# First logits of a fused attention and two-layer expert kernel moved to another PSUM bank and to the end of a pair's scores, and half of the first loads issued by ScalarE

## The chip, the cores and the metric

The kernel runs on one core of a Trainium2 chip. The metric is the time of one execution in microseconds (us), as the device measures it; the kernel before has a median of 680.31 us over 3 runs (679.55 to 680.96).

## What is computed

Three stages follow each other; everything is float32.

```python
# q, k, v: (4, 12, 448, 64): 4 batches, 12 heads, 448 tokens
scores = matmul(q, k.transpose(0, 1, 3, 2)) / sqrt(64) - log(448)
x = matmul(1 / (1 + exp(-scores)), v)          # sigmoid attention
x = x.transpose(0, 2, 1, 3).reshape(1792, 768)
x = ((x @ w_a) * (x @ w_b)) @ w_out            # 768 -> 1536 -> 768
logits = x @ phi                               # (1792, 32): 8 experts, 4 slots each
d = softmax(logits, axis=0)                    # over the tokens
slots = d.T @ x                                # (32, 768)
y = relu(slots @ w1[e]) @ w2[e]                # per expert e
c = softmax(logits, axis=1)                    # over the slots
out = c @ y
```

## The kernel before, in words

**Work.** Two heads make a pair, so there are 24 pairs `g`, six to a batch. For each pair `load_qkv` (lines 120 to 151) loads k, q and v; k and q are transposed and split into a high and a low part (`emit_TK`, `emit_TQ`), on TensorE for the early pairs (line 170, evicted by VectorE and ScalarE) and on VectorE from pair 13 on (line 166). `emit_S` (197 to 212) computes scores in four chunks of 112 keys, each chunk as two PSUM tiles (one per head) with three matmuls each; ScalarE turns each tile into a sigmoid (line 211). `emit_PV` (216 to 222) multiplies the eight sigmoid tiles of a pair with v in sixteen matmuls, and `emit_x` evicts the result (on ScalarE, line 244, from batch 1 on).

**Order.** Nothing is scheduled by a compiler: each engine runs its instructions in the order in which the code issues them. `att` (253 to 294) is the generator that sets that order for attention. For pair 12 and later it emits: the k/q split of pair `g + 1`; chunk 0 of pair `g`; the PV product of pair `g - 1` and its eviction; then chunks 1, 2 and 3 of pair `g`. After every `yield` of `att` the main loop (1021 to 1029) lets one `fill_step` run, which advances a queue of filler generators by one step.

**The filler around the change.** When batch 0's product of the second stage is done, `first_LG` (868 to 878) is put into that queue. It transposes four 128 by 512 blocks on TensorE (`group`, line 529, evicted by VectorE at 531) and runs `LG(0)`: `logits(0)` (line 775) waits for the flag `run["done"]`, then emits one matmul that adds four partial logits (line 783), the maximum over the tokens (787, 793, VectorE), the exponential (802, ScalarE, which loads another table for it and the sigmoid's table again afterwards), a copy of the logits (807, VectorE); later steps transpose the two results (819, 825) and multiply the exponentials with the second stage's result (836, 96 matmuls).

**PSUM.** `ms` tiles (lines 64 to 68) are general tiles with 2 banks; score tiles have the tags `sc` (4 banks) and, for chunk 2, `ab` (2 banks). From pair 13 on (`GT0`) the first head's tile of chunk 0 is an `ms` tile; from pair 12 on the PV product's tile is one too.

**Start.** `load_qkv(0)` loads k and q of pair 0 head by head, all issued by SyncE (line 150), then v; then `consts` sets up constants; then pairs 1 and 2 are loaded. TensorE's first work is the transposes of k and q of pair 0 (line 170).

**End.** From about 480 us on the expert weights (48 MB) stream in through a ring of slots (line 979).

```python
for cost in att_g:
    if not run.pop("trans", False):
        fill_step()
    run.pop("done", None)
```

Of the kernel before, what the change touches and what calls it, by code (L numbers as in the profile page):

```python
# [18 lines left out]
B, H, S, D = 4, 12, 448, 64  # L19
DM, FF, NS, NE, F = 768, 1536, 32, 8, 1024  # L20
C = 4
# [14 lines left out]
def body(ctx, tc, q, k, v, w_a, w_b, w_out, phi, w1, w2, out):  # L36
    nc = tc.nc
    pe, act, dve, pool, sp = nc.tensor, nc.scalar, nc.vector, nc.gpsimd, nc.sync
# [15 lines left out]
    run = {}  # L54

    def ps_tile(tag, shape, bufs):
        return psp.tile(shape, F32, tag=tag, name=tag, bufs=bufs)
# [6 lines left out]
    def ms(shape=(128, S)):  # L64
        tags = banks[run["banks"]]
        tag = tags[run["ms"] % len(tags)]
        run["ms"] += 1
        return ps_tile(tag, list(shape), 4 if tag == "sc" else 2)
# [51 lines left out]
    def load_qkv(g, names):  # L120
        if g >= B * NP:
            return
        b, p = divmod(g, NP)
        for src, nm, n in ((k, "k", 3), (q, "q", 3), (v, "v", 3)):
            if nm not in names:
                continue

            if g >= GT0:
                if nm == "v":
                    t = atp.tile([T, 2, C, D], F32, tag="vn", name="vn", bufs=n)  # L130
                    sp.dma_start(out=t, in_=src[b, 2 * p:2 * p + 2].rearrange("h (c p) d -> p h c d", c=C))
                else:
                    t = atp.tile([128, 2 * C * D], F32, tag=nm + "n", name=nm + "n", bufs=n)
                    t = t[:, :S].rearrange("p (n d) -> p n d", d=32)
                    for j in range(4):
                        sp.dma_start(out=t[32 * j:32 * j + 32],
                                     in_=src[b, 2 * p + j // 2][:, j % 2 * 32:j % 2 * 32 + 32].rearrange(
                                         "(n t) d -> t n d", t=32))
                qkv_t[nm, g] = t
                continue  # L140
            s = src[b, 2 * p:2 * p + 2].rearrange(
                "h (c p) d -> p h c d" if nm == "q" else "h (p c) d -> p h c d", c=C)
            if nm == "v":
                t = atp.tile([T, 2, C, D], F32, tag="vn", name="vn", bufs=n)
                sp.dma_start(out=t, in_=s)
            else:
                t = atp.tile([128, 2 * C * D], F32, tag=nm + "n", name=nm + "n", bufs=n)
                t = t[:T].rearrange("p (c h d) -> p c h d", c=C, h=2)
                for h in range(2):
                    sp.dma_start(out=t[:, :, h], in_=s[:, h])  # L150
            qkv_t[nm, g] = t

    stk = {}
# [21 lines left out]
    def emit_TK(g):  # L175
        if g >= B * NP:
            return
        if g >= GT0:
            for nm in "kq":
                split_heads(g, nm, transposed(g, nm), dve.tensor_copy)  # L180
                load_qkv(g + 3, nm)
            return
        tk = transposed(g, "k")
        if not g:
            tq = transposed(g, "q")
        split_heads(g, "k", tk, dve.tensor_copy)
        if not g:
            split_heads(g, "q", tq, act.copy)

    def emit_TQ(g):  # L190
        if g >= B * NP:
            return
        split_heads(g, "q", transposed(g, "q"), dve.tensor_copy)
# [3 lines left out]
    def emit_S(g, chunks):  # L197

        (kh, kl), (qh, ql) = stk[g]["k"], stk[g]["q"]
        for c in chunks:  # L200
            ab = (g < NP or g > 2 * NP) and c == 2
            sc = [ms((T, S)) if g >= GT0 and c == 0 and not h else ps_tile("ab" if ab else "sc", [T, S], 2 if ab else 4)
                  for h in range(2)]
            cs = slice(c * T, (c + 1) * T)
            for i, (kx, qx) in enumerate(((kh, qh), (kl, qh), (kh, ql))):
                for h in range(2):
                    r = slice(64 * h, 64 * h + 64)
                    pe.matmul(sc[h], kx[r, cs], qx[r], start=(i == 0), stop=(i == 2))  # L208
            for h in range(2):
                a = atp.tile([T, S], F32, tag="a", name="a", bufs=11)  # L210
                act.activation(a, sc[h], AF.Sigmoid, bias=nlog[:T], scale=1.0 / math.sqrt(D))  # L211
                a_t[g, h, c] = a
# [3 lines left out]
    def emit_PV(g, cs):  # L216
        if cs[0] == 0:
            pv_t[g] = ps_tile("sc", [128, S], 4) if g < 2 * NP else ms()
        for c in cs:
            for h in range(2):  # L220
                pe.matmul(pv_t[g][64 * h:64 * h + 64], qkv_t["v", g][:, h, c, :], a_t.pop((g, h, c)),  # L221
                          start=(c == 0), stop=(c == C - 1))
# [15 lines left out]
    def emit_x(g):  # L238
        pv = pv_t.pop(g)
        qkv_t.pop(("v", g))  # L240
        b, kk = divmod(g, NP)
        if b:
            xt[g] = raw_x(b, kk)
            act.copy(xt[g], pv)
        else:
            xh = x0p.tile([128, S], F32R, tag=f"xh{kk}", name=f"xh{kk}")
            xl = x0p.tile([128, S], F32R, tag=f"xl{kk}", name=f"xl{kk}")
            act.activation(xh, pv, AF.Copy)
            dve.tensor_tensor(xl, pv, xh.bitcast(F32), op=ALU.subtract)
            xt[g] = (xh, xl)  # L250
        load_qkv(g + 3, "v")

    def att():

        emit_TK(0)
        yield 860
        for g in range(B * NP + 1):
            more = g < B * NP
            dense = g < NP or g >= 2 * NP
            first = ((0, 1) if g == 0 else (0, 2) if g == B * NP - 1 else (0,) if dense else ()) if more else ()  # L260
            if g:
                emit_TK(g + 1)
                yield 430
            for c in first:
                emit_S(g, (c,))
                run["done"] = True
                yield 800
            if g:
                if g < NP and more:
                    emit_TQ(g + 1)  # L270
                    yield 430
                emit_PV(g - 1, (0, 1, 2, 3))
                emit_x(g - 1)
                yield 3200
            else:
                emit_TK(g + 1)
                yield 430
            if not more:
                return
            if not dense:  # L280
                emit_S(g, (0, 1))
                yield 1600
                emit_TQ(g + 1)
                yield 430
                emit_S(g, (2, 3))
                yield 1600
            else:
                if not g:
                    emit_TQ(g + 1)
                    yield 430  # L290
                for c in range(C):
                    if c not in first:
                        emit_S(g, (c,))
                        yield 800

    PAIR = 860 + 4 * 800 + 3200
# [478 lines left out]
    def logits(b):  # L775
        while not b and not run.pop("done", False):
            yield
        if b == B - 1:
            project(b, 2, 3)
        lf = ms()  # L780
        if b == B - 1:
            pe.matmul(lf, wphi[:, :4].rearrange("p j s -> p (j s)"), gT[b, KF - 1], start=True, stop=False)
        pe.matmul(lf, selF.rearrange("p j s -> p (j s)"), lp[b], start=b < B - 1, stop=True)
        if b:
            yield
        mx = col()
        dve.tensor_reduce(mx, lf, axis=AX.X, op=ALU.max)
        nm = col()
        if b:
            mn = col()  # L790
            dve.tensor_tensor(mn, run["m"], mx, op=ALU.max)
            mx, m0 = mn, run["m"]
        dve.tensor_scalar(nm, mx, -1.0, None, op0=ALU.mult)
        if b:
            dm = col()
            dve.tensor_tensor(dm, m0, mx, op=ALU.subtract)
        run["m"] = mx
        if b:
            yield
        sm = col()  # L800
        ls, d = run["lsd"]
        act.activation(d, lf, AF.Exp, bias=nm, accum_out=sm)
        if b:
            al = col()
            act.activation(al, dm, AF.Exp)
            run["al"] = al
        (act.copy if b else dve.tensor_copy)(ls, lf)
        yield
        if b:
            sn = col()  # L810
            dve.scalar_tensor_tensor(sn, run["s"], al, sm, op0=ALU.mult, op1=ALU.add)
            sm = sn
        run["s"] = sm
# [290 lines left out]
    for what in order0:  # L1104
        i = what[1]
        h, n, f0 = (0, 4, 4 * i) if i < 3 else (1, 6, 6 * (i - 3))
# [18 lines left out]
    for n in range(0, len(order1), 4):  # L1125
        _, g, x, _ = order1[n]
# [51 lines left out]
    for h, (c0, w) in enumerate(COLS):  # L1178
# [4 lines left out]
        t = ms((128, w))  # L1183
# [41 lines left out]
```

## Time and profile before

| what | value |
|---|---|
| median of 3 runs | 680.31 us (679.55 to 680.96) |
| the profiled execution | 683.6 us, of which the span of the profile is 681.8 us |
| TensorE busy in the span | 639.4 us (94%) |
| VectorE / ScalarE / GpSimdE busy | 397.3 / 294.0 / 311.8 us |
| moved by DMA | 154.25 MB, 226 GB/s over the span |
| mean granted clock of TensorE | 0.983 of full speed |
| chain that ended last | TensorE 77%, DMA 13%, ScalarE 3%, VectorE 2%, issue 2% |

The profile is one execution. In its rows PE is TensorE's matmuls, PEld its weight loads, DVE is VectorE, ACT is ScalarE, POOL is GpSimdE, SP is SyncE; SPq and ACTq are the sequencers that issue DMAs. `L783` is line 783 of the kernel. A wait in brackets is idle time of the engine just before the row, with what ended it. The chain that ended last is followed back from the last instruction: at each step to what released it, or to the instruction before it on its engine. The 1.8 us between the span and the profiled execution lie outside of the profile.

### The profile page before, as it was taken

The page shows a single profiled execution, that of the slowest core. Times are in us where ns is not written, and L with a number is a line of the kernel's source. Part 1 is how long each engine was busy: PE and PEld are TensorE (multiplying, and loading weights), DVE is VectorE, ACT ScalarE, POOL GpSimd, SP SyncE. Part 2 cuts the span into 40 slices and gives each one's busy share as a digit, 9 for nine tenths or more (in the row PEclk, how much of TensorE's full clock was granted, in tenths as well). Part 3 has the DMA queues.
Part 4 walks back from the last instruction along what each step waited for, and adds up shares of the span by engine and source line. Part 5 has one row for each costly group of instructions (what it writes and reads, how often), then busy time and mean ns, then how long its engine had stood idle before and what let it go on. Part 6 is the DMA issues. An engine that isn't in the chain of part 4 may idle for free.

```text
span 681.8 us, 10900 instructions
## 1 busy us (share of the span) xinstructions
PE 639.4 (94%) x4035; PEld 455.0 (67%) x4035; DVE 397.3 (58%) x565; ACT 294.0 (43%) x531; POOL 311.8 (46%) x236
## 2 busy tenths in 40 slices
PE   6999999997999899999999999999999998996693
PEld 4556777775676455568998898898879895441131
DVE  4775899996994648929887767754233422210022
ACT  4888778776683568874333233201210002110021
POOL 0233677666773207819997675742344442000000
PEclk9999999999999899999999999999999999999888
DMA  9997999999997346310214242341999999999998
GB/s 192 278 275 190 289 308 304 282 274 295 288 293 198 71 83 115 60 48 3 91 47 115 79 101 93 102 124 40 280 382 366 403 370 332 412 414 417 405 354 276
DMA packets 150292, 154.25 MB, mean 226 GB/s; under 512 B 81792, under 2 KB 126688, under 8 KB 147168
## 3 DMA queue, kind: packets, MB, share of 16 engines
q1 hardware_dynamic: 145600, 151.61, 71.3%
q10 hardware_dynamic: 4640, 1.95, 1.1%
q8 instruction: 32, 0.52, 0.3%
q14 instruction: 20, 0.16, 0.1%
HBM read 126.36 MB, written 27.17 MB: 225 GB/s over the span
## 4 chain that ended last, share of the span: by engine, by line
PE 77%; DMA 13%; ACT 3%; DVE 2%; issue 2%; POOL 1%; SPq 0%; DVEq 0%; ACTq 0%; POOLq 0%
PE ab L565 24%; PE sc L745 15%; DMA e<-in_moe_w 8%; PE ab L745 8%; PE sc L208 6%; PE sc L221 5%; PE ms L221 4%; DMA out<-w 3%; PE ms L170 2%; PE ms L836 2%; PE ab L208 1%; PE ms L493 1%; ACT a L211 1%; DMA gkp<-in_moe_w 1%; PE sc L1193 1%
## 5 line engine op out<-in xcount | busy, mean ns | idle before, releaser
L367 POOL TENSOR_TENSOR w<-gk,cy 128x768 int32<-128x768 int32 x36 | 66.7, 1853 | 91.1 <-DVE gk L362 57.6
L211 ACT ACTIVATE a<-sc,sums 112x448 f32<-112x448 f32 x147 | 84.4, 642 | 12.2 <-PE sc L208 11.9
L565 PE MATMUL ab<-t,wh 128*128 128x448 f32 x288 | 65.1, 371 | 0.0
L565 PEld LDWEIGHTS ab<-t,wh 128*128 128x128 f32 x288 | 53.4, 188 | 6.1 <-issue 1.3
L463 POOL TENSOR_TENSOR wl<-wr,wh 128x768 fp32r<-128x768 f32 x16 | 29.5, 1841 | 49.9 <-DVE wh L462 25.7
L463 POOL TENSOR_TENSOR wl<-w,wh 128x768 fp32r<-128x768 f32 x24 | 47.0, 1960 | 2.5 <-ACT wh L462 2.5
L572 ACT COPY misc<-ab 128x448 f32<-128x448 f32 x24 | 12.7, 529 | 80.7 <-PE ab L565 80.7
L1156 PE MATMUL ab<-e,gk 128*32 128x384 f32 x240 | 33.1, 573 | 10.7 <-DMA e<-in_moe_w 10.6
L360 DVE TENSOR_SCALAR mf<-gk 128x768 f32<-128x768 f32 x36 | 34.0, 943 | 14.3 <-ACT gk L349 14.1
L221 PE MATMUL sc<-a,vn 112*64 112x448 f32 x192 | 39.1, 546 | 1.0 <-ACT a L211 1.0
L221 PE MATMUL ms<-a,vn 112*64 112x448 f32 x192 | 38.7, 545 | 0.2 <-ACT a L211 0.2
L575 DVE TENSOR_TENSOR misc<-misc,ab 128x448 f32<-128x448 f32 x24 | 14.7, 614 | 36.8 <-PE ab L565 36.8
L208 PE MATMUL sc<-qh,kh 64*112 64x448 f32 x147 | 35.4, 431 | 0.7 <-ACT qh L158 0.6
L565 PE MATMUL ab<-xh,wl 128*128 128x448 f32 x144 | 35.4, 383 | 0.0
L361 DVE TENSOR_SCALAR gk<-mf 128x768 uint32<-128x768 uint32 x36 | 34.3, 953 | 1.2
L565 PE MATMUL ab<-xh,wh 128*128 128x448 f32 x144 | 34.9, 378 | 0.0
L565 PE MATMUL ab<-xl,wh 128*128 128x448 f32 x144 | 34.5, 375 | 0.0
L565 PE MATMUL ab<-t,wl 128*128 128x448 f32 x144 | 34.3, 373 | 0.0
L629 POOL TENSOR_TENSOR wx<-wr,wx 128x384 fp32r<-128x384 f32 x29 | 32.3, 1115 | 3.5 <-ACT wx L628 3.4
L628 ACT CAST wx<-T 128x384 fp32r<-128x384 f32 x21 | 10.8, 513 | 53.4 <-DVE T L650 33.9
L629 POOL TENSOR_TENSOR wx<-T,wx 128x384 fp32r<-128x384 f32 x23 | 24.8, 1080 | 16.9 <-ACT wx L628 15.6
L1195 DVE COPY o<-sc 112x384 f32<-112x384 f32 x11 | 5.6, 551 | 46.0 <-PE sc L1193 45.9
(458 smaller groups left out, 1514.4 us busy)
## 6 DMA issues: line engine op xcount, KB each, us to landing
e<-in_moe_w SPq DMA_DIRECT2D x23, 1024.0 KB, 8.8
e<-in_moe_w SPq DMA_DIRECT2D x23, 768.0 KB, 15.1
wr<-ab SPq DMA_DIRECT2D x14, 768.0 KB, 4.6
ab<-w SPq DMA_DIRECT2D x24, 384.0 KB, 6.9
vn<-in_v SPq DMA_DIRECT2D x24, 224.0 KB, 4.1
gk<-gk SPq DMA_DIRECT2D x24, 224.0 KB, 4.6
e<-in_moe_w SPq DMA_DIRECT2D x14, 384.0 KB, 8.8
wr_cv<-in_moe_w_a SPq DMA_DIRECT2D x6, 768.0 KB, 7.4
```

Of the source, the lines that this page charges most:

```text
L208: pe.matmul(sc[h], kx[r, cs], qx[r], start=(i == 0), stop=(i == 2))
L211: act.activation(a, sc[h], AF.Sigmoid, bias=nlog[:T], scale=1.0 / math.sqrt(D))
L221: pe.matmul(pv_t[g][64 * h:64 * h + 64], qkv_t["v", g][:, h, c, :], a_t.pop((g, h, c)), start=(c == 0), stop=(c == C - 1))
L360: dve.tensor_scalar(mf, m, LOW, HIGH, op0=ALU.max, op1=ALU.min)
L361: dve.tensor_scalar(mi, mf.bitcast(U32), 3, 0x3FFFFFFF, op0=ALU.logical_shift_left, op1=ALU.bitwise_and)
L367: pool.tensor_tensor(thirds(w), m.bitcast(I32), thirds(cy_t.pop(x)), op=ALU.add)
L463: pool.tensor_tensor(wl, t, wh.bitcast(F32), op=ALU.subtract)
L565: pe.matmul(t, w[:, kk * 128:(kk + 1) * 128], xt[b * NP + kk][xi], start=(s == 0 and kk == 0), stop=(s == 2 and kk == KD - 1))
L575: dve.tensor_tensor(g, g, t, op=ALU.mult)
L629: pool.tensor_tensor(w[:, 1], t, w[:, 0].bitcast(F32), op=ALU.subtract)
L745: pe.matmul(t, w[:, wi, k * 128:(k + 1) * 128], xs[ORDER[m], k][xi], start=(s == 0 and k == 0), stop=(s == 2 and k == 2))
L1156: pe.matmul(sps[h][32 * j:32 * j + 32], hT[:, 2 * x + i, 2 * j + g], ring[order2[n + j]][0][:, i, c0:c0 + w], start=(g == 0 and x == 0 and ...
```

## The change

Two places. In `load_qkv`, for pair 0 alone, the second head's k and q are issued by ScalarE's DMA queue, the first head's by SyncE's as before. In the logits of batch 0, the PSUM tile is of the tag `ab` and no longer an `ms` tile, and the flag that `logits(0)` waits for is set after the last of chunks 1 to 3 (only then true) and no longer after the chunks that come ahead of the PV product.

```diff
                 for h in range(2):
-                    sp.dma_start(out=t[:, :, h], in_=s[:, h])
+                    (sp if g or not h else act).dma_start(out=t[:, :, h], in_=s[:, h])
...
             for c in first:
                 emit_S(g, (c,))
-                run["done"] = True
                 yield 800
...
                 for c in range(C):
                     if c not in first:
                         emit_S(g, (c,))
+                        run["done"] = c == C - 1
                         yield 800
...
-        lf = ms()
+        lf = ms() if b else ps_tile("ab", [128, S], 2)
```

What moves at the start, on SyncE (kn and qn are the tiles of k and q; a row with x2 is both heads):

```order
 L1221 UNCONDITIONAL_BRANCH
-L150 DMA kn<-in_k 112x4x64 x2
-L150 DMA qn<-in_q 112x4x64 x2
+L150 DMA kn<-in_k 112x4x64
+L150 DMA qn<-in_q 112x4x64
 L145 DMA vn<-in_v 112x2x256
 L150 DMA kn<-in_k 112x4x64 x2
```

SyncE issues two DMAs fewer ahead of v of pair 0 and of everything behind it; ScalarE issues the same two ahead of its first table load.

What moves on TensorE in pair 13, beside which `logits(0)` runs (L208 are scores, L221 the PV product of pair 12, L529 the block transposes, L783 the logits):

```order
 L208 MATMUL sc<-ql,kh 112x448
-L783 MATMUL ms<-misc,selF 128x448
 L221 MATMUL ms<-a,vn 64x448 x8
 L208 MATMUL sc<-qh,kh 112x448 x2
 L208 MATMUL sc<-qh,kl 112x448 x2
 L208 MATMUL sc<-ql,kh 112x448 x2
-L529 MATMUL ms<-ident,misc 128x128 x4
 L208 MATMUL ab<-qh,kh 112x448 x2
 L208 MATMUL ab<-qh,kl 112x448 x2
```

The logits matmul is gone from ahead of the PV product, and with it the four transposes that stood behind chunk 1. Where they stand now, with the waits of each row, between chunk 3 of pair 13 and the PV product of pair 13 (a_2545 is the first sigmoid tile of pair 13; ms_2632 and sc_2633 are chunk 0 of pair 14):

```order
L783 MATMUL ab_2606<-misc_95,selF_90 128x448 [waits DVE_49,Activation_49]
L208 MATMUL ms_2632<-qh_2524,kh_2514 112x448 [waits DVE_49,PE_49]
L208 MATMUL sc_2633<-qh_2524,kh_2514 112x448
...
L208 MATMUL sc_2633<-ql_2525,kh_2514 112x448
L529 MATMUL ms_2644<-ident_89,misc_95 128x128 [waits PE_49]
L529 MATMUL ms_2644<-ident_89,misc_95 128x128 x3
L221 MATMUL ms_2650<-a_2545,vn_2087 64x448 [waits DMAHW3_49,Activation_49]
```

The other transposes, the steps of lines 819 and 825 and the 96 matmuls of line 836 follow about a pair later than before, all still ahead of the PV product of pair 15, as before. On ScalarE the exponential moves with them (L211 are sigmoids, L244 the eviction of the PV product of pair 12):

```order
 L211 ACTIVATE a<-sc,sums 112x448
+L244 COPY r_2562<-ms 128x448
+L211 ACTIVATE a<-sc,sums 112x448 x2
+L211 ACTIVATE a<-ab,sums 112x448 x2
+L211 ACTIVATE a<-sc,sums 112x448 x2
 L802 ACT_TABLE_LOAD
-L802 ACTIVATE ls_d,sums<-ms,sums 128x448
-L244 COPY r_2568<-ms 128x448
+L802 ACTIVATE ls_d,sums<-ab,sums 128x448
 L211 ACT_TABLE_LOAD
```

Before, the two table loads stood ahead of the sigmoids of chunks 1 to 3 of pair 13, around the eviction of the PV product; now they stand behind those, and ahead of the sigmoids of chunk 0 of pair 14.

## Rows read from the trace of the kernel before

**Rows 1.** The page, busy time, share of the span and instructions of each engine.

```profile
PE 639.4 (94%) x4035; PEld 455.0 (67%) x4035; DVE 397.3 (58%) x565; ACT 294.0 (43%) x531; POOL 311.8 (46%) x236
```

**Rows 2.** Waits of TensorE, 0 to 240 us: us in total, times, longest us.

```profile
PE ms L170 <- ACT wT L393: 2.8, 3, 2.2
...
PE ms L170 <- DMA qn<-in_q: 0.2, 1, 0.2
PE ms L221 <- ACT a L211: 0.2, 1, 0.2
```

**Rows 3.** Timeline of SyncE, 0 to 14 us: start us, us, what.

```profile
0.73 1.36 SPq L150 DMA_DIRECT2D kn<-in_k  x2
2.14 1.15 SPq L150 DMA_DIRECT2D qn<-in_q  x2
```

**Rows 4.** The chain that ended last, 0 to 60 us: start us, us, what.

```profile
2.80 3.37 DMA qn<-in_q
...
6.30 0.99 PE ms L170 x4
...
15.77 0.54 PE ms L170 x4
```

**Rows 5.** Busy time by stretch at the start; last columns granted clock, DMA share, GB/s.

```profile
3.00:4.00 1.00, 0.00 (x0) 0.00 (x0) 0.00 (x0) 0.00 (x0) 0.00 (x0) 1.00 0.41 94
4.00:5.00 1.00, 0.00 (x0) 0.00 (x0) 0.00 (x0) 0.00 (x0) 0.00 (x0) 1.00 1.23 264
```

**Rows 6.** Timeline of TensorE, 220 to 234 us.

```profile
221.03 1.02 PE L783 MATMUL ms<-misc,selF 128*128 128x448 f32 x2 [1.23 <-ACT a L211]
221.97 3.23 PE L221 MATMUL ms<-a,vn 112*64 112x448 f32 x16
...
227.72 0.66 PE L529 MATMUL ms<-ident,misc 128*128 128x128 f32 x4 [1.72 <-ACT r L244]
...
230.20 1.97 PE L529 MATMUL ms<-ident,misc 128*128 128x128 f32 x8
```

**Rows 7.** Timeline of ScalarE, 218 to 232 us.

```profile
225.22 1.28 ACT L802 ACT_TABLE_LOAD   x1 [3.72 <-issue]
...
227.14 0.52 ACT L244 COPY r<-ms 128x448 f32<-128x448 f32 x1
227.68 1.28 ACT L211 ACT_TABLE_LOAD   x1
228.97 1.16 ACT L211 ACTIVATE a<-sc,sums 112x448 f32<-112x448 f32 x2
```

**Rows 8.** Busy time by stretch around the logits; third column from the end granted clock.

```profile
229.60:233.00 3.40, 3.40 (x18) 2.19 (x16) 1.49 (x3) 2.63 (x6) 2.11 (x2) 0.58 0.00 0
```

**Rows 9.** Timeline of an undisturbed pair, 250 to 257 us, TensorE and ScalarE.

```profile
250.14 3.23 PE L221 MATMUL ms<-a,vn 112*64 112x448 f32 x16
...
255.31 1.16 ACT L211 ACTIVATE a<-ab,sums 112x448 f32<-112x448 f32 x2
...
255.93 3.23 PE L221 MATMUL ms<-a,vn 112*64 112x448 f32 x16
256.34 1.18 ACT L211 ACTIVATE a<-sc,sums 112x448 f32<-112x448 f32 x2
```

**Rows 10.** The chain that ended last, 216 to 252 us: score chunks.

```profile
228.37 0.79 PE ab L208 x6
229.16 1.11 PE sc L208 x6
...
248.39 0.61 PE ab L208 x6
```

**Rows 11.** Busy time by stretch, 480 to 560 us; columns as in Rows 5.

```profile
480.00:560.00 80.00, 80.00 (x556) 67.57 (x556) 26.09 (x49) 6.76 (x15) 32.77 (x18) 1.00 1.02 365
```

**Rows 12.** The chain that ended last, over the whole span, two pieces.

```profile
122.55 8.95 DMA out<-w
...
590.32 11.05 DMA e<-in_moe_w
```

## Prediction

> **What bounds the kernel now.** I read the page first. TensorE is busy for 639.4 of 681.8 us [rows 1]: whatever keeps it waiting counts. Next come its waits up to 240 us: 2.8 us in three waits at the weight conversion [rows 2], and 1.2 and 1.7 us around the first logits, the brackets in its timeline [rows 6]. At the start it has nothing to do until k and q of pair 0 have landed [rows 4]. From there on the reader should see that nothing makes TensorE wait: it is busy for all of 480 to 560 us, while the DMA engines are full [rows 11], and from 590 us the chain is one load of expert weights after another [rows 12]. That stream starts when TensorE gets to its place in the program, so a microsecond won or lost before 480 us moves the end by one, and I count both places of the change in full.
>
> **The first loads.** SyncE takes 1.36 us to issue k and 1.15 us to issue q of pair 0 [rows 3]. The last of the four DMAs is issued at 2.80 and lands 3.37 us later, at 6.17; the transposes of q start at 6.30 [rows 4]. With two queues the second k is issued at 0.73 with the first, the second q at some 1.4. ScalarE's own first work, a table load and one activation, slips by 1.3 us, and the eviction that it has to be ready for comes 4 us later: no cost. Three estimates of the gain:
> - by latency: 2.80 - 1.4 = 1.4 us;
> - by bytes: the four loads are 458 KB. At 94 GB/s between 3 and 4 us the engines are fed slower than they work (0.41 busy), at 264 GB/s one microsecond later they are full [rows 5]. With two issuers the 264 GB/s are there from the first byte, at some 2.2 us: 458 KB by 3.9 us in place of 4.9, so 1.0 us;
> - by TensorE: the transposes of k, as long as q's 0.99 us [rows 4], stand ahead of q's. The second k is issued half of 1.36 us earlier, so they start 0.7 us earlier; q's then lose at most that and the 0.2 us for which they wait now [rows 2]: 0.9 us.
>
> The least of the three binds: I take 0.9 us, with 0 and 1.4 as ends (0 if the engines are full anyway). Everything behind on SyncE is issued 1.25 us earlier too, so the loads of pairs 1 and 2 stay ahead. The row speaks for a gain; the Trainium skill's "DMA: Bandwidth & Descriptors" (section "Issuing engines are not separate DMA queues") says that DMAs from several issuers share the same 16 engines, and that only issue time is saved. By that rule the gain cannot exceed the 1.25 us of issue; with engines already full it would be nothing.
>
> **The logits' matmul.** Before, L783 stands ahead of the PV product of pair 12 and waits 1.23 us for a sigmoid [rows 6]. The PV product then needs that bank's neighbour; in the changed order it takes the bank itself and waits for the same sigmoid, so the 1.23 us stay and it starts at 221.03 in place of 221.97. The 0.94 us of L783 are not gone, they come later.
>
> The waits that go: four block transposes wait 1.72 us for the eviction of the PV product [rows 6], which is late because the exponential stands ahead of it on ScalarE, with a table load on each side (225.22 and 227.68 [rows 7]). Another 0.2 us go at the next PV product [rows 2]. Together 1.9 us.
>
> The waits that come, from the undisturbed pair [rows 9], whose times are counted from its PV product at 250.14 and put on 221.03:
> - L783 takes the bank of the first `ab` score tile. That one's sigmoid starts 5.17 us after the PV product and takes 0.64 (two overlap in the 1.16 of the row): 226.84. TensorE is through with chunk 3 after 5.79 less 0.6 us, at 226.2. Wait: 0.7 us. L783 ends at 227.8.
> - Behind it stand chunk 0 of pair 14 (0.79 us [rows 10]) and one block transpose step (0.66 us [rows 6]): TensorE is done at 229.25. Next is the PV product of pair 13. It is the third `ms` tile in a row, and there are two banks: it needs that of chunk 0, whose sigmoid must have read it. ScalarE finishes the sigmoids of chunk 3 at 6.20 + 1.18 = 7.38 us, at 228.4. Then come table, exponential, table: from the first load at 225.22 to the first activation at 228.97 they take 3.75 us before, of which 0.5 is the eviction in between [rows 7], so 3.25. With one sigmoid of 0.64 behind, the bank is free at 232.4. **Wait: 3.2 us.** The maximum on VectorE is hidden, it takes 0.8 us and has the 1.3 us of the table load.
> - One pair later the sigmoids trail the PV product of pair 14 by some 0.4 us, as the pace of 1.16 us for two makes it.
>
> So 4.3 us come and 1.9 go: +2.4. Given back: score chunks behind their like take 0.61 us, behind other work 0.79 [rows 10]; the filler splits two chunks fewer: -0.4. Net **+2.0 us**.
>
> **The clock.** After the 1.72 us wait the granted clock falls: 0.58 in 229.6 to 233.0 [rows 8], so it is at 1.2 GHz for most of it, 2.4 GHz elsewhere. The eight transposes there take 1.97 us where two steps of 0.66 took 1.32 [rows 6], a chunk 1.11 instead of 0.79 [rows 10], the next some 0.15 more: 1.1 us in all. Behind 3.2 us of wait I expect the same again. Ends: 0 (1.1 us less than the sum), and 1.7 if work fills the whole stretch (0.6 more).
>
> **The tables.** At 227.68 the table load starts 0.02 us behind the copy, and 1.29 us later the next activation runs [rows 7]: 1.28 is all that a switch costs there. The Trainium skill's "ScalarE: Activation LUTs" (section "What ACT_TABLE_LOAD costs") gives 1283 ns for the load and some 1380 ns of drain ahead of it, 2.66 us in all, which this row contradicts. By that rule the first load, now right behind a queue of sigmoids, and the second would be dearer by 2.8 us in the sum.
>
> **Sum.** -0.9 + 2.0 = +1.1 us. The profiled execution, 683.6 us, goes to 684.7, with a span near 682.9. It is 3.3 us longer than the median of the runs shown; the difference of +1.1 carries over: 680.31 + 1.1 = **681.4 us**. A measurement of this kernel can tell some 0.2%, 1.4 us, from no change: faster is below 678.95, slower above 681.67.
>
> **The rivals.**
> - *The start's gain is used up, slower.* DMA engines that are full from 4 us on set the pace of the early stages: a conversion waits 8.95 us for a write to land [rows 12], and TensorE waits 2.8 us there [rows 2]. If the stream that those writes queue in does not start earlier, the 0.9 us is lost at 122 to 168 us, and the logits' +2.0 stand alone: 682.3. Decides: whether TensorE reaches 170 us earlier than before. For: the share of 1.23 [rows 5]. Against: TensorE works without a wait for most of the way.
> - *The clock rises sooner at the start.* The first transposes take 0.99 us, those at 15.77 take 0.54 [rows 4]: the start runs at the low clock. If the high one comes not 0.9 but 3.9 us sooner, the 3 us more take half the time: -1.5, 679.9. For: TensorE's work is denser sooner. Against: no row shows what it would take.
> - *The PV product of pair 13 does not wait for the new sigmoid.* The wait list names ScalarE, not which activation. If it is an earlier one, 3.2 us of wait and the low clock behind it (1.1) don't arise: +1.1 becomes -3.2, 677.1. For: it is what moving L783 into another bank would be good for. Against: the same pattern of three tiles in two banks waits for that sigmoid before [rows 2].
> - *Nothing of weight moves.* Full engines at the start and a shorter queue on ScalarE at the logits: 680.3.
> - *The drain of the tables is paid:* 681.4 + 2.8 = 684.2, the time that the quoted rule gives.
>
> **How the numbers follow.** The forecast has 0.40, of it 0.24 within 0.2% and 0.16 slower (the full low stretch alone takes it to 682.0). Gain used up: 0.20, of it 0.18 slower. Clock sooner: 0.16, of it 0.05 faster. No wait at the PV product: 0.10, faster. Nothing: 0.10. Drain: 0.04, slower. Faster 0.15, same 0.47, slower 0.38. The range leaves out the case at 677.1, the drain, and the tails: 679.0, a microsecond below the sooner clock, to 683.0, the used-up gain with the full low stretch (682.3 + 0.6).
>
> **What would show it.** Right: q's transposes near 5.4 us; the PV product of pair 12 earlier by the start's gain and another 0.9; a row of that of pair 13 with a wait of some 3 us ended by ACT L211; two table loads with the exponential between them right behind six sigmoids; a stretch of low clock behind. Wrong: q's transposes at 6 us or later; no wait over 1 us on TensorE between 215 and 245 us; or TensorE at 170 us no earlier than before, which is the first rival.

## The result, and the profile after

| what | before | changed |
|---|---|---|
| median (beside each other) | 680.96 us (679.55 to 683.23, 5 runs) | 685.3 us (684.77 to 687.06, 5 runs) |
| ratio | | 1.0066, 95% interval 1.0044 to 1.0087 |
| the profiled execution, its span | 683.6 us, 681.8 us | 685.3 us, 683.5 us |

The changed kernel is slower by 4.3 us, with 3.0 to 5.9 as the interval. (A ratio here and below, and its interval, is worked out from the runs and not exactly that of the two medians.) The forecast was 681.4 us, and its range ended at 683.0.

The two profiled executions differ by only 1.7 us, because that of the kernel before was 2.6 us longer than its median. So two traces set side by side do not show the whole difference here; what they show has to be read stretch by stretch.

On the page of the changed kernel (busy time, share of the span and instructions of each engine) TensorE is busy for 1.4 us more than before, in a span 1.7 us longer [rows 1]:

```profile
PE 640.8 (94%) x4035; PEld 454.3 (66%) x4035; DVE 398.9 (58%) x565; ACT 293.9 (43%) x531; POOL 312.1 (46%) x236
```

**The logits.** TensorE's waits from 0 to 240 us (us in total, times, longest), against [rows 2]:

```profile
PE ms L221 <- ACT a L211: 4.4, 2, 3.2
...
PE ms L170 <- DMA qn<-in_q: 1.3, 1, 1.3
...
PE ab L783 <- ACT a L211: 0.5, 1, 0.5
```

TensorE's timeline of the changed kernel from 218 to 262 us, the PV products of pairs 12, 13, 14, 15 and 16, the logits and the block transposes, against [rows 6]:

```profile
218.92 3.23 PE L221 MATMUL ms<-a,vn 112*64 112x448 f32 x16 [1.23 <-ACT a L211]
...
224.71 1.02 PE L783 MATMUL ab<-misc,selF 128*128 128x448 f32 x2 [0.55 <-ACT a L211]
...
226.46 0.66 PE L529 MATMUL ms<-ident,misc 128*128 128x128 f32 x4
230.27 4.92 PE L221 MATMUL ms<-a,vn 112*64 112x448 f32 x16 [3.16 <-ACT a L211]
...
235.92 1.09 PE L529 MATMUL ms<-ident,misc 128*128 128x128 f32 x8
...
240.69 3.23 PE L221 MATMUL ms<-a,vn 112*64 112x448 f32 x16 [0.50 <-ACT a L211]
...
250.44 3.23 PE L221 MATMUL ms<-a,vn 112*64 112x448 f32 x16
...
256.22 3.23 PE L221 MATMUL ms<-a,vn 112*64 112x448 f32 x16
```

ScalarE's timeline of the changed kernel from 218 to 242 us, against [rows 7]:

```profile
225.06 1.18 ACT L211 ACTIVATE a<-sc,sums 112x448 f32<-112x448 f32 x2
226.25 1.28 ACT L802 ACT_TABLE_LOAD   x1
227.55 0.63 ACT L802 ACTIVATE ls_d<-ab,sums 128x448 f32<-128x448 f32 x1
...
228.29 1.28 ACT L211 ACT_TABLE_LOAD   x1
229.58 0.63 ACT L211 ACTIVATE a<-ms,sums 112x448 f32<-112x448 f32 x1
```

The chain is complete in these two views. ScalarE works through the six sigmoids of pair 13, then two table loads with the exponential between them, and the first sigmoid after that (229.58 to 230.21) is the one that reads the `ms` tile of chunk 0 of pair 14. The PV product of pair 13 starts 0.06 us behind it: it is the third `ms` tile in a row and needs that tile's bank. Behind its 3.16 us of wait the granted clock (third column from the end) is low, against [rows 8]:

```profile
230.40:234.00 3.60, 3.60 (x12) 1.15 (x14) 2.34 (x5) 0.34 (x1) 0.00 (x0) 0.53 0.46 74
```

That is mostly 1.2 GHz, and the product takes 4.92 us in place of 3.23.

**The start.** The issues of SyncE and of ScalarE, and the transposes of k and q, against [rows 3, 4]:

```profile
0.73 0.72 SPq L150 DMA_DIRECT2D kn<-in_k  x1
1.50 0.59 SPq L150 DMA_DIRECT2D qn<-in_q  x1
2.14 0.49 SPq L145 DMA_DIRECT2D vn<-in_v  x1
2.68 1.25 SPq L150 DMA_DIRECT2D kn<-in_k  x2
```

```profile
0.73 0.72 ACTq L150 DMA_DIRECT2D kn<-in_k  x1
1.49 0.88 ACTq L150 DMA_DIRECT2D qn<-in_q  x1
```

```profile
4.24 0.98 PE L170 MATMUL ms<-ident,kn 112*128 112x112 f32 x4 [4.24 <-DMA kn<-in_k]
6.48 1.01 PE L170 MATMUL ms<-ident,qn 112*128 112x112 f32 x4 [1.26 <-DMA qn<-in_q]
```

The transposes of k in the kernel before:

```profile
5.09 0.98 PE L170 MATMUL ms<-ident,kn 112*128 112x112 f32 x4 [5.09 <-DMA kn<-in_k]
```

In these two traces k is there 0.85 us earlier, q 0.2 us later than before, although its second half was issued at 1.49 and no longer at 2.80.

### The profile page after: what moved, and what is told of

It is laid out like the page before. It is cut to its first block, busy times and chain, and to the rows that moved or that the text cites. A ratio compares the mean times of both kernels' runs of the same rounds, so it can differ in the third digit from the quotient of the medians.

```text
span 683.5 us, 10901 instructions
## 1 busy us (share of the span) xinstructions
PE 640.8 (94%) x4035; PEld 454.3 (66%) x4035; DVE 398.9 (58%) x565; ACT 293.9 (43%) x531; POOL 312.1 (46%) x236
## 4 chain that ended last, share of the span: by engine, by line
PE 52%; DMA 9%; ACT 1%; DVE 1%; issue 1%; POOL 1%; SPq 0%; DVEq 0%; ACTq 0%
PE sc L745 15%; PE ab L565 13%; DMA e<-in_moe_w 8%; PE ab L745 8%; PE ms L221 5%; PE sc L208 2%; PE ms L836 2%; DMA gkp<-in_moe_w 1%; PE ms L493 1%; PE sc L1110 1%; ACT a L211 1%; PE sc L1193 1%; PE ab L1156 1%; PE ab L208 1%; PE sc L1130 1%
## 5 line engine op out<-in xcount | busy, mean ns | idle before, releaser
L211 ACT ACTIVATE a<-sc,sums 112x448 f32<-112x448 f32 x147 | 84.2, 643 | 13.7 <-PE sc L208 13.3
L221 PE MATMUL ms<-a,vn 112*64 112x448 f32 x192 | 40.4, 565 | 4.9 <-ACT a L211 4.9
L221 PE MATMUL sc<-a,vn 112*64 112x448 f32 x192 | 39.1, 546 | 1.0 <-ACT a L211 1.0
L208 PE MATMUL sc<-qh,kh 64*112 64x448 f32 x147 | 34.8, 424 | 0.7 <-ACT qh L158 0.6
```

## Landmarks of all traces

The experiments below are read by four numbers of each trace: the start of q's transposes, of the first PV product, of the PV products of pair 11 and of pair 16. The last difference holds all that moves around the logits.

| kernel | q | first PV | PV 11 | PV 16 | 11 to 16 |
|---|---|---|---|---|---|
| before | 6.30 | 16.23 | 204.39 | 255.93 | 51.54 |
| before, again | 6.30 | 15.60 | 200.86 | 251.52 | 50.66 |
| loads_only | 6.20 | 15.53 | 202.92 | 254.47 | 51.55 |
| k_by_act | 5.73 | 14.69 | 202.18 | 254.06 | 51.88 |
| logits_only | 6.03 | 14.63 | 200.50 | 254.43 | 53.93 |
| changed | 6.48 | 15.48 | 202.28 | 256.22 | 53.94 |
| changed, again | 6.73 | 16.13 | 203.31 | 257.23 | 53.92 |
| ms_bank_new_place | 6.29 | 15.16 | 202.38 | 256.14 | 53.76 |
| later_transposes | 6.14 | 15.75 | 202.69 | 252.92 | 50.23 |
| chunk0_sc | 6.52 | 16.37 | 204.02 | 254.45 | 50.43 |
| ab_bank_old_place | 6.67 | 16.26 | 204.12 | 255.31 | 51.19 |
| best_a | 5.77 | 14.79 | 202.37 | 251.78 | 49.41 |
| best_c | 5.72 | 14.34 | 201.19 | 250.05 | 48.86 |

From the PV product of pair 16 to L1110 (578.42 us in the kernel before), a product with weights of the stream at the end, it takes 322.4 to 322.8 us in twelve of these traces and 323.1 in the other (the second of the changed kernel): what is lost before 256 us arrives there in full. From the PV product of pair 16 to the end of the span it takes 425.4 to 426.1 us in ten traces, and 427.3 to 427.7 in three: both of the changed kernel and that of chunk0_sc. Up to the PV product of pair 11, executions of one kernel differ by more than any part of this change is worth.

## Experiments

**before_again.** The kernel before, unchanged.

> The kernel before, unchanged, for a second trace of it. Its profiled execution took 683.6 us, 2.6 more than its median of 680.96 over the five runs beside the changed kernel. Theory A (that execution was an unlucky one: TensorE's clock rose late, at 14.0 us, and it waited 0.95 us for a converted weight at 163 us): ratio 0.998 to 1.002, and the new trace reaches the first logits (L783, 221.03 us there) one to two microseconds earlier, with the clock up before 14 us or no wait of 0.95 us at L392. Rival B (the first loads' change gave the 2.1 us by which the changed kernel's trace is ahead at 218 us): the new trace reaches L783 at 221.0 +- 0.3 us again.

Measured: 680.82 us (12 runs), ratio 1.0007, 0.999 to 1.0023. The trace, TensorE from 210 to 256 us, and a window of it:

```profile
217.77 1.02 PE L783 MATMUL ms<-misc,selF 128*128 128x448 f32 x2 [1.22 <-ACT a L211]
...
224.45 0.66 PE L529 MATMUL ms<-ident,misc 128*128 128x128 f32 x4 [1.71 <-ACT r L244]
226.43 1.09 PE L529 MATMUL ms<-ident,misc 128*128 128x128 f32 x8
```

```profile
226.00:229.60 3.60, 3.03 (x26) 1.89 (x22) 2.40 (x5) 3.60 (x8) 2.44 (x3) 1.00 0.01 1
```

Theory A: the same kernel reaches the logits 3.3 us earlier than in its first trace, so the 2.1 us by which the changed kernel's trace is ahead there need no cause in the change. And in this execution the clock does not fall behind the 1.71 us of wait: eight transposes take 1.09 us and not 1.97 [rows 6], and the stretch is 0.88 us shorter. Across the runs beside this and the next three kernels the kernel before has a median of 681.06 us (31 runs), 0.75 above the 680.31 from which the forecast started.

**loads_only.** The first loads as changed, the logits as before.

```diff
-                    sp.dma_start(out=t[:, :, h], in_=s[:, h])
+                    (sp if g or not h else act).dma_start(out=t[:, :, h], in_=s[:, h])
```

> The change of the first loads alone. In the changed kernel q's transposes started at 6.48 us in place of 6.30, with a wait of 1.26 us for the DMA. Theory A (the second issuer gains nothing, since the DMA engines are the limit when q lands): 680.3 to 681.7 us, ratio 0.999 to 1.001, q's transposes at 6.3 to 6.6 us. Rival B (it gains the 0.9 to 2.1 us by which the changed kernel's trace is ahead from 14 and from 163 us on): 678.9 to 680.1 us, ratio 0.997 to 0.9985. Rival C (it costs, because later transfers are disturbed): 682 us or more.

Measured: 681.76 us (12 runs), ratio 1.0011, 0.9995 to 1.0026. ScalarE's issue, its time to landing (last column, us) and the transposes of q:

```profile
1.50 0.88 ACTq L150 DMA_DIRECT2D qn<-in_q  x1
```

```profile
qn<-in_q SPq DMA_DIRECT2D x3, 112.0 KB, 4.2
...
qn<-in_q ACTq DMA_DIRECT2D x1, 112.0 KB, 4.7
```

```profile
6.20 1.01 PE L170 MATMUL ms<-ident,qn 112*128 112x112 f32 x4 [0.93 <-DMA qn<-in_q]
```

Theory A: no gain, and no loss that can be told from none. The second q issued 1.3 us earlier takes 4.7 us to land in place of 3.37 [rows 4].

**logits_only.** The logits as changed (bank and place), the loads as before.

```diff
-                run["done"] = True
...
+                        run["done"] = c == C - 1
...
-        lf = ms()
+        lf = ms() if b else ps_tile("ab", [128, S], 2)
```

> The logits' move alone: ab bank and new place. Theory A (it carries the whole loss: 3.2 us of wait at the PV product of pair 13 with a low clock behind it, against 1.9 us that go): 683.3 to 685.5 us, ratio 1.0035 to 1.0065, and the waits of 0.5, 3.2 and 0.5 us at L783 and L221 stand in the trace. Rival B (the loads give 2 us, so that the logits cost over 6): 686.5 us or more. Rival C (half of the loss is where a low clock falls at L1110, 578 us, and not the logits): 682 to 683 us, and a trace without that low clock gains nothing else on the changed kernel's.

Measured: 683.94 us (8 runs), ratio 1.0048, 1.003 to 1.0066. TensorE, 214 to 258 us:

```profile
228.49 4.92 PE L221 MATMUL ms<-a,vn 112*64 112x448 f32 x16 [3.16 <-ACT a L211]
```

Theory A: the wait and the slow product are there to the hundredth, and this part alone costs 2.9 us (2.0 to 4.5).

**later_transposes.** As logits_only, with one filler step skipped behind chunk 0 of pair 14, so that one `ms` tile less stands ahead of the PV product of pair 13.

```diff
-                emit_S(g, (c,))
+                emit_S(g, (c,)); run.update({"trans": True} if g == 2 * NP + 2 else {})
                 yield 800
```

> As logits_only, but one filler step is skipped between chunk 0 of pair 14 and the PV product of pair 13, so that the four block transposes (one ms tile) come behind that product and it gets the other ms bank, not the one that chunk 0's sigmoid has to read first. Theory A (the 3.2 us are that wait for the bank, and the low clock behind it is its consequence): the wait is gone, no low clock near 231 us, 3.2 to 5 us faster than logits_only, 678 to 681 us. Rival D (the PV product waits for its own sigmoids or for its data, not for the bank): within 1 us of logits_only. Rival E (the wait moves one product on, to that of pair 14, whose bank the transposes then hold up): 1 to 2 us faster than logits_only, with a wait of 1 us or more there.

Measured: 681.75 us (12 runs), ratio 1.0011, 0.9996 to 1.0026. TensorE, and the granted clock behind it:

```profile
226.86 3.23 PE L221 MATMUL ms<-a,vn 112*64 112x448 f32 x16
230.68 0.66 PE L529 MATMUL ms<-ident,misc 128*128 128x128 f32 x4 [0.59 <-ACT a L211]
...
236.88 3.23 PE L221 MATMUL ms<-a,vn 112*64 112x448 f32 x16 [0.78 <-ACT a L211]
```

```profile
230.00:234.00 4.00, 3.41 (x28) 2.37 (x28) 3.75 (x8) 3.34 (x7) 0.00 (x0) 1.00 0.33 53
```

The wait of 3.2 us and the low clock are gone together, and the stretch is 3.7 us shorter than in logits_only, as theory A has it. The median gives back 2.2 us only, less than it forecast; waits of 0.59 and 0.78 us come behind (rival E's kind, under its size), but the 3.7 us hold them already, so why the median shows less stays open.

**chunk0_sc.** As logits_only, with pair 14's first tile in `sc`.

```diff
-            sc = [ms((T, S)) if g >= GT0 and c == 0 and not h else ps_tile("ab" if ab else "sc", [T, S], 2 if ab else 4)
+            sc = [ms((T, S)) if g >= GT0 and g != 2 * NP + 2 and c == 0 and not h else ps_tile("ab" if ab else "sc", [T, S], 2 if ab else 4)
```

> As logits_only (ab bank, new place), but the first tile of chunk 0 of pair 14 is an sc tile and no ms tile, so that the PV product of pair 13 is no longer the third ms tile in a row: its bank is one that nothing on ScalarE has to read first. Nothing else moves up to there. Theory A (the 3.2 us are the wait for that bank): the product starts right behind the block transposes, no low clock behind it, and of ScalarE's 3.25 us only what the next pairs cannot hide is left: the stretch from the PV product of pair 11 to that of pair 16 takes 47.5 to 50.5 us, where logits_only took 53.9 and the kernel before 51.5 and 50.7; 677.5 to 681 us. Rival D (the product waits for its own sigmoids): 53 us and 683 us or more. Rival E (the same microseconds come back at the next products): waits of 1 us or more ended by ScalarE at the PV products of pairs 14 and 15, 50.5 to 52 us, 680.5 to 682 us.

Measured: 682.48 us (12 runs), ratio 1.0013, 0.9994 to 1.0032. TensorE, 214 to 258 us:

```profile
228.19 0.66 PE L529 MATMUL ms<-ident,misc 128*128 128x128 f32 x4
228.78 3.23 PE L221 MATMUL ms<-a,vn 112*64 112x448 f32 x16
```

The order of the work is that of logits_only; only the bank differs, and the product no longer waits. This settles that the 3.2 us are a wait for the bank, and not for the product's own sigmoids (rival D). The stretch of 50.43 us is where theory A put it, 3.5 us shorter than in logits_only. The median lies above its 681 us, and only 1.5 us below that of logits_only. This trace loses 1.65 us elsewhere (at L1110, below), but one execution does not account for a median of twelve; that difference stays open.

**ab_bank_old_place.** The kernel before with the new bank alone.

```diff
-        lf = ms()
+        lf = ms() if b else ps_tile("ab", [128, S], 2)
```

> The kernel before with the logits in an ab bank at the old place, ahead of the PV product of pair 12. Theory A (the place costs, the bank would have helped: L783 runs within the 1.2 us wait that is there anyway, and the block transposes no longer stand in the bank that the late eviction of the PV product has to clear): the 1.7 us wait at L529 is gone or below 0.5, the stretch from the PV product of pair 11 to that of pair 16 takes 48 to 50.5 us, 678 to 680.5 us. Rival F (ScalarE's tables come at the same place and TensorE waits for the sigmoids behind them, wherever the banks are): 50.5 to 51.6 us as before, 680.5 to 681.5 us. Rival G (the bank itself costs, chunk 2 needs it while the exponential still reads it): a wait at L208 ab, 682 us or more.

Measured: 681.46 us (12 runs), ratio 1.0007, 0.9993 to 1.0021. TensorE, 214 to 258 us:

```profile
224.71 0.66 PE L529 MATMUL ms<-ident,misc 128*128 128x128 f32 x4
...
227.69 0.45 PE L208 MATMUL ab<-qh,kh 64*112 64x448 f32 x1 [1.94 <-DVE ls_d L807]
```

Theory A fails. The 1.72 us at L529 are gone, and 1.94 us come at chunk 2 of the same pair, whose bank the logits still occupy until VectorE has copied them. It is rival G's wait, and with the 0.94 us that are saved ahead of the PV product the stretch and the time are rival F's. At the old place the bank moves the wait and saves nothing that the median shows.

**ms_bank_new_place.** The new place with the old bank, against logits_only.

```diff
-        lf = ms() if b else ps_tile("ab", [128, S], 2)
+        lf = ms()
```

> The new place with the logits still in an ms tile. Theory A (at this place there is one ms tile too many for two banks, with either bank for the logits; the place costs, the ab bank saves nothing much): within 1 us of logits_only, 683 to 685 us, with waits of 3 us or more in sum ended by ScalarE at L529 or at the PV product of pair 13. Rival H (the ab bank is what costs, by the wait at L783 for chunk 2's sigmoid and by the order of tiles behind it): 680.5 to 682 us.

Measured: 686.06 us (6 runs), ratio 1.0069, 1.0048 to 1.0089. TensorE, 214 to 258 us:

```profile
229.08 0.66 PE L529 MATMUL ms<-ident,misc 128*128 128x128 f32 x4 [3.08 <-DVE ls_d L807]
230.37 4.76 PE L221 MATMUL ms<-a,vn 112*64 112x448 f32 x16 [0.63 <-ACT a L211]
```

Theory A in the trace: 3.7 us of wait at the same point and the slow product behind it, with either bank. So the loss belongs to the place: the exponential and its tables stand behind ScalarE's sigmoids and ahead of what frees the banks. Here 3.08 us end with VectorE's copy of the logits (228.40 to 229.02), which itself waits for the exponential, and 0.63 us with the sigmoid behind the second table load. The median is 2.1 us above logits_only, which the stretch (53.76) does not show; the intervals overlap.

**k_by_act.** The kernel before, with the second k of pair 0 alone by ScalarE.

```diff
-                    sp.dma_start(out=t[:, :, h], in_=s[:, h])
+                    (sp if g or not h or nm == "q" else act).dma_start(out=t[:, :, h], in_=s[:, h])
```

> The kernel before with the second k of pair 0 alone issued by ScalarE; both q stay on SyncE's queue, ahead of v and of pair 1's loads. In loads_only ScalarE's q was issued at 1.49 us in place of 2.80 and landed at 6.16, as late as before, while v and the next pair's k, issued 1.2 us earlier on the other queue, landed 0.5 us earlier. Theory A (two queues share the engines, so what is issued earlier on the one takes the other's share; q has to stand ahead of the later loads in one queue): the second q lands at 5.2 to 5.8 us and its transposes start by 5.9; the time 680 to 681 us, since 0.5 us of start is below what a median of these runs shows. Rival I (the bytes up to q take until 6.2 us whoever issues them): q's transposes at 6.1 to 6.4 us again.

Measured: 681.57 us (12 runs; 681.22 for the kernel before beside it), ratio 0.9994, 0.9978 to 1.001. The transposes of q:

```profile
5.73 0.98 PE L170 MATMUL ms<-ident,qn 112*128 112x112 f32 x4 [0.43 <-DMA qn<-in_q]
```

Theory A in the trace: with both q in the queue that also holds v and pair 1, and ahead of those, q is there 0.57 us earlier than before; its second load, issued at some 2.1 us, lands 3.4 us later. In all three traces with these loads q's transposes start at 5.72 to 5.77 us and the first PV product at 14.3 to 14.8. In the three with the change's own loads (6.20 to 6.73) it starts at 15.5 to 16.1; the seven with the old loads have 14.6 to 16.4. The gain is at the start of the trace; the median by itself does not show it.

This run changes two things against loads_only: v and pair 1 stand behind both q, and the second q no longer goes through ScalarE's queue. That queue is a rival of its own. Where both engines issued a load of the same size at the same time, that of ScalarE landed later in every trace: the second k after 3.4 to 3.6 us and the first after 2.9 to 3.0 (six traces), the second q after 4.7 to 5.2 us and the first after 3.1 to 4.1 (the three traces with the change's own loads). No run separates the two causes.

**after_again.** The changed kernel once more.

> The changed kernel, unchanged, once more: the median of 685.3 us rests on five runs, and the two parts alone gave 681.76 (loads) and 683.94 us (logits), 0.7 and 2.9 us above the kernel before. Theory A (the parts add up, the loads are worth nothing or a few tenths either way; the time swings by two to three us with the place where TensorE's clock changes and with DMA landings before 200 us): 683.5 to 685.3 us, ratio 1.0035 to 1.0062; in the trace the PV product of pair 13 waits 3.2 us again and the stretch from the PV product of pair 11 to that of pair 16 takes 53.0 to 54.0 us again. Rival J (the two parts together cost something that neither costs alone, as the slow weight product at 578 us, 5.74 in place of 4.08 us): 685.3 us or more, and L1110 takes 5.7 us again.

Measured: 684.97 us (12 runs), ratio 1.0051, 1.003 to 1.0073. The kernel before has 681.27 us beside it (29 runs): 3.7 us, close to the 0.7 and 2.9 of the parts. TensorE at L1110 in this trace and in the first one of the changed kernel:

```profile
580.34 4.08 PE L1110 MATMUL sc<-e,misc 128*32 128x512 f32 x48 [0.24 <-ACT misc L902]
```

```profile
578.68 5.74 PE L1110 MATMUL sc<-e,misc 128*32 128x512 f32 x48 [0.23 <-ACT misc L902]
```

Theory A, and not rival J: the slow L1110 does not come in every execution of the changed kernel. It is in its first trace and in that of chunk0_sc, and in none of the other eleven. Both of these have the logits at the new place, but so have six traces without it; whether the change makes it more frequent is not shown. This trace loses 0.6 us ahead of L1110 in its place, and 1.1 us in the last stage, where one load of expert weights takes 16.27 us on the chain that ended last (15.04 to 15.15 for such loads in the first trace of the kernel before).

**best_a, best_c.** The logits as changed; the first tile of chunk 0 in `sc` for pairs 13 and 14 (best_c: 13 to 15); the loads of k_by_act. The diff of best_a against logits_only:

```diff
-            sc = [ms((T, S)) if g >= GT0 and c == 0 and not h else ps_tile("ab" if ab else "sc", [T, S], 2 if ab else 4)
+            sc = [ms((T, S)) if g > GT0 + 1 and c == 0 and not h else ps_tile("ab" if ab else "sc", [T, S], 2 if ab else 4)
...
-                    sp.dma_start(out=t[:, :, h], in_=s[:, h])
+                    (sp if g or not h or nm == "q" else act).dma_start(out=t[:, :, h], in_=s[:, h])
```

> The logits as changed (ab bank, new place), the first tile of chunk 0 of pairs 13 and 14 in sc and not in ms, so that neither the PV product of pair 12 (1.23 us of wait in every trace so far) nor that of pair 13 (3.2 us) has to wait for a sigmoid to clear its bank; and of pair 0's loads the second k alone by ScalarE (q's transposes at 5.73 in place of 6.30 us). Theory A: no wait at the PV products of pairs 12 and 13, the stretch from the PV product of pair 11 to that of pair 16 at 48.8 to 50.0 us where the kernel before took 50.7 and 51.5; with 0.5 us at the start 678.3 to 680 us, ratio 0.996 to 0.9985. Rival E (ScalarE's 3.25 us come back as waits for sigmoids in sc banks at L208): such waits of 1 us or more, 50.5 us or more, 680.5 us or more.

> As best_a, with pair 15's first tile of chunk 0 in sc as well, for the 0.5 us for which the PV product of pair 14 waits behind the other changes. Theory A: 0.3 to 0.6 us less in the same stretch than best_a, 678 to 680 us. Rival E: no change against best_a, because that product then waits for its own sigmoids.

Measured: best_a 679.18 us (12 runs), ratio 0.9965, 0.9943 to 0.9987; best_c 679.05 us (12 runs), ratio 0.9963, 0.9948 to 0.9977. TensorE of best_a, 214 to 258 us:

```profile
217.97 3.23 PE L221 MATMUL ms<-a,vn 112*64 112x448 f32 x16
...
226.10 3.23 PE L221 MATMUL ms<-a,vn 112*64 112x448 f32 x16
...
236.25 3.23 PE L221 MATMUL ms<-a,vn 112*64 112x448 f32 x16 [0.48 <-ACT a L211]
```

and of best_c, the PV product of pair 14:

```profile
234.46 3.23 PE L221 MATMUL ms<-a,vn 112*64 112x448 f32 x16
```

Theory A for both: the 1.23 us ahead of the PV product of pair 12 are gone too, which stood in every trace before these but that of ab_bank_old_place (there the logits' matmul fills most of them), and these two beat both kernels, the one before by 2.1 and 2.2 us. What the loads and what the tiles give of that, the medians do not separate. The stretch of best_c is 0.55 us shorter than best_a's, as expected; the medians do not tell the two apart.

## Why the prediction was wrong, point by point

**What held.** TensorE bounds, and a microsecond before 480 us moves the end by one (322.4 to 323.1 us from pair 16 to L1110 in all traces). The PV product of pair 12 starts 0.94 us earlier from pair 11 on (16.64 us behind it, before 17.58). The three waits were forecast as 0.7, 3.2 and 0.4 us and are 0.55, 3.16 and 0.50, each ended by the activation that was named; those that were to go, 1.72 and 0.19, went. chunk0_sc and later_transposes show that the large one is the wait for the bank. Two of its terms were rounded up in the working: 226.84 less 226.2 is 0.64 and not 0.7, and 228.4 + 3.25 + 0.64 is 232.3 and not 232.4, so the large wait comes out at 3.1. The table loads of the changed kernel take 1.28 us each, start 0.01 to 0.02 us behind the instruction ahead of them and end 0.01 to 0.02 us ahead of the next (226.25 and 228.29 us above, and a third at 477.75). "ScalarE: Activation LUTs" of the Trainium skill (section "What ACT_TABLE_LOAD costs") adds some 1380 ns of drain to a switch, which these three do not show on either side.

**The first loads: -0.9 forecast, nothing measured.** The step that failed is the one that took the four loads by themselves, by latency, by bytes and by TensorE, and then counted it a good that "Everything behind on SyncE is issued 1.25 us earlier too". In the three traces of these loads the second q, issued 1.3 us earlier, takes 4.7 to 5.2 us to land in place of 3.37, and its transposes start at 6.20 to 6.73 us where the seven traces with the old loads have 6.03 to 6.67. v and pair 1's k are now issued from 2.14 us on in another queue and no longer stand behind that q. Put back behind it, in k_by_act, q's transposes start 0.57 us earlier than before. That v and pair 1 use the gain up is theory A; that ScalarE's queue is later by itself is as open (k_by_act). The first rival had the shared engines, but saw the loss at 122 to 168 us. "DMA: Bandwidth & Descriptors" (the Trainium skill, section "Issuing engines are not separate DMA queues") says that loads of several issuers run on the same engines. The traces agree: from 4 to 5 us both queues together moved 249 GB/s in the first trace of the changed kernel, SyncE's alone 264 before [rows 5].

**The logits: +2.0 forecast, +2.9 measured alone (2.0 to 4.5), +2.4 to +3.3 in the stretch, against the two traces of the kernel before.** The mechanism was right, one term mis-sized: "Behind 3.2 us of wait I expect the same again" set the clock's loss equal on both sides. It is 1.69 us in the new order (4.92 against 3.23), in three traces of three, and so at the end of 1.7 that the prediction gave. In the old order it makes the stretch 0.88 us longer (51.54 against 50.66; 1.22 in k_by_act, 51.88), and only in the executions in which it comes (three traces of four with the old logits). The estimate of 1.1 was taken from one execution that had it; the end of 0.6 more was given, the case of a loss before that is not always there was not. The 0.4 given back is some 0.7: 4.21 - 1.91 + 0.81 of waits and clock are 3.11, and the stretch shows 2.40.

One cause of the 1.72 us that went was overlooked. In the kernel before, the maximum that the exponential needs stands on VectorE behind the split of the next k and q (its timeline from 218 to 232 us):

```profile
224.27 0.62 DVE L787 TENSOR_REDUCE sums<-ms 128x1 f32<-128x448 f32 x1
```

The logits had been there since some 222.0 us. ScalarE sat idle for 3.72 us and began the first table load at 225.22, 0.15 us after VectorE was through with the maximum and its sign (225.07) [rows 7]; that made the eviction late. In ab_bank_old_place the load again starts 0.15 us after them (224.96 after 224.81), though the PV product had ended at 223.99. In the changed kernel the maximum starts 0.04 us after the logits (225.77). Had it run 2.2 us earlier at the old place, the load and the exponential would have been through before the PV product ended at 225.20 [rows 6], by these durations. That is an estimate; no run moves the maximum alone.

**The base.** The sum was put on 680.31 us, the median of three runs; 31, 29 and 29 further ones, beside the three sets of experiments, give 681.06, 681.22 and 681.27. That is 0.75 to 0.96 us of the miss.

**The sum and the range.** Of the 3.9 us between 681.4 and 685.3 the base has some 0.9, the loads 0.9, the logits 0.9 (2.9 in place of 2.0). The rest is about 1.2 us, and both traces of the changed kernel lose some 1.5 us behind the PV product of pair 16 that ten of the other eleven do not lose: 1.66 us at L1110 in the one, 0.6 us ahead of it and 1.1 us at a load of weights in the other. Neither loads_only nor logits_only has such a loss, so whether it belongs to the change or to the execution stays open. Without those 1.2 us the changed kernel would be at 684.1 us, 3.1 above the kernel before, which is the lower end of the first interval (3.0 to 5.9) and inside the second (2.0 to 5.0). The range held each bound by itself, the used-up start with the full low stretch, but not the base, and left out what all three do on one side. That the time swings by several microseconds from execution to execution (679.2 to 683.9 us in 31 runs of the kernel before), which the three runs shown only hinted at, should have widened it at its upper end.

**The rivals.** The used-up start had the right time for the loads, at another place. Its sign, TensorE earlier at 170 us or not, decides nothing: at the PV product of pair 11 the changed kernel stands at 202.28 and 203.31 us, between the 200.86 and 204.39 of the kernel before. An earlier clock at the start cannot be told either, since with q at 6.30 us in both traces of the kernel before its first PV product starts at 16.23 and at 15.60. The 3.16 us of wait rule out the case without that wait.

## What to carry to other kernels

Before work with a table switch is moved on ScalarE, ask which sigmoid (or other eviction) comes right behind it and whose PSUM bank that one frees: at the end of a pair the switch stood ahead of the very activation that the next PV product needed, and either bank for the moved tile left some 3 us of wait in place, while one tile taken out of the rotation removed it. Before loads are split over two DMA queues, ask what less urgent load is brought forward with them, and how late the loads of the second queue land: here the second q, split off, was no earlier, and with both q ahead of the other loads in one queue and only k split off it was 0.57 us earlier. A term read off one execution, a stretch of low clock above all, belongs into a sum only with the question whether it is there in every execution.

## What was not expected of the hardware

- ScalarE took 0.88 us to issue the load of q for which SyncE took 0.59, in each of the three traces; for the load of k both took 0.72 to 0.73.
- Stretches of low clock fall differently in executions of one and the same kernel. The first trace of the kernel before has one at 229 us, its second none there. In the first trace of the changed kernel one falls right on L1110:

```profile
578.60:582.10 3.50, 3.42 (x19) 0.81 (x23) 0.24 (x1) 0.03 (x1) 0.00 (x0) 0.51 0.95 329
```

  and costs 1.66 us (5.74 in place of 4.08). Behind the 3.16 us of wait one came in all three traces that have it.
- The same kernel reaches the PV product of pair 11 at 204.39 us in one execution and at 200.86 in another, nearly as much as the whole change costs.
